# Attention with squared relu, then a gated feed-forward block: the first batch's queries loaded and transposed by themselves, and the order of the early work changed

## The chip, the core and the metric

The kernel runs on one core of a Trainium2 chip. A core has a matrix engine (TensorE, PE in the profile; its weight loads are the row PEld), a vector engine (VectorE, DVE), a scalar engine (ScalarE, ACT), a general engine (GpSimd, POOL) and a synchronising engine (SyncE, SP). Each has its own instruction stream and works through it in order; semaphores between the streams do the waiting. Data comes from HBM into the on-chip SBUF by DMA; matrix products land in PSUM. The metric is the device time of one execution, in microseconds (us).

## The reference

There are 8 batches (B), 12 heads (H), a sequence of 448 (S), a head width of 64 (D); the model width DM is 768 and the feed-forward width F is 1536.

```
scores = scale * (q @ k.T)               # per batch and head, 448 x 448
attn   = max(scores, 0)**2 / 448
x      = attn @ v                        # heads side by side: 3584 x 768
xn     = x / sqrt(mean(x*x) + 1e-6) * rms_g
out    = (silu(xn @ w_gate) * (xn @ w_val)) @ w_out      # 3584 x 768
```

All inputs are float32; the kernel converts them to bfloat16 while it loads them.

## The kernel before

**Loads.** Every input is loaded by a DMA that GpSimd issues (`load_q`, `load_k`, `load_kx`, `load_v`, `load_vx`, `load_gv`, lines 89 to 136). Queries come in pairs of batches: partitions 0 to 63 of the tile `qld` hold the even batch (e = 0), partitions 64 to 127 the odd one (e = 1), and `load_q` issues one DMA for each. Keys and values are split into the first 384 rows (`kld`, `vld`) and the last 64 (`kxld`, `vxld`). Lines 138 to 167 set the order of the first loads: heads 0 and 1, then 2 and 3, then 4 to 7, then 8 to 11, each time the queries of both batches of the pair; then the first 256 columns of the gate and value weights (`load_gv(0, 256)`), the keys of batch 1, more weights, the values of batch 1, more weights. Later loads are issued from inside the loop.

**Transposes.** For the scores, queries and keys are needed with the head width on the partitions. `transposes(n)` does one pair of heads j of batch b, with n = 6b + j. For the first pair of batches, and for the queries of the second pair, it does so on TensorE: 14 small matmuls against an identity for the queries (`psQ`, both batches of the pair at once), 6 and 2 for the keys (`psK`), then one copy by VectorE each (lines 206 and 218) into `QT` and `KT`. Later batches are transposed by DMAs that SyncE issues.

**The loop.** Step m (lines 464 to 486) works on a third of a batch, four heads: b, t = m divided by 3. `scores(m, slots)` makes seven slots of scores; of each slot TensorE makes four matmuls in pairs (line 265), ScalarE takes the relu out of PSUM (line 273, two PSUM buffers), VectorE squares (line 274). `attend(m - 1)` multiplies the seven squared slots of the step before with the values (line 297), ScalarE scales the result (line 309) and VectorE squares it (line 310). Slots 0 to 2 use head pair 2t, slots 3 to 5 head pair 2t + 1.

**The feed-forward work.** After a batch's three steps `norm(b)` sums the squares over the model width on TensorE (line 331), takes the root on ScalarE (line 339) and appends eleven steps to a list `bg`: four reciprocals (line 352), six scalings (line 355), which write the six parts of `xn`, and `ready`, which calls `gates`. `gates` appends 24 pieces to the list `pieces`: for each of 12 blocks of the width F a `gate` piece (six matmuls of line 382, then silu) and a `val` piece (six matmuls of line 396, then a product on VectorE, line 403). After an odd batch, `outproj` appends 14 output pieces (line 425).

**What sets the order.** The whole order is written out by hand. Every engine runs its instructions in the order in which the loop emits them. `fill(us)` adds its budget to a running `debt`, emits pieces while the debt is positive (a gate or value piece counts as 1.13, an output piece as 1.97), and after each piece it runs one step of `bg`. With no piece left, it runs three steps of `bg` and sets the debt to zero. Three fills a step share a rate of 7.8 in steps 0 to 6 and of 13.8 from step 7 on.

Of the kernel before, what the change touches and what calls it, by code (L numbers as in the profile page):

```python
# [9 lines left out]
BF16 = mybir.dt.bfloat16  # L10
# [5 lines left out]
def kernel(  # L16
# [11 lines left out]
    nc = tc.nc  # L28
    P = nc.NUM_PARTITIONS

    B, H, S, D = q.shape
# [5 lines left out]
    XT0 = NCH * P  # L37
    XK = S - XT0

    NU = 7  # L40
    HALF = S // NU
# [4 lines left out]
    ND = HP // 2  # L46
# [5 lines left out]
    wpool = ctx.enter_context(tc.tile_pool(name="weights", bufs=1))  # L52
    ldpool = ctx.enter_context(tc.tile_pool(name="ld", bufs=2))
    tpool = ctx.enter_context(tc.tile_pool(name="tsb", bufs=2))
    rpool = ctx.enter_context(tc.tile_pool(name="relu2", bufs=10))
    xpool = ctx.enter_context(tc.tile_pool(name="xT", bufs=2))
    hpool = ctx.enter_context(tc.tile_pool(name="hT", bufs=14))
    opool = ctx.enter_context(tc.tile_pool(name="ostage", bufs=2))
    psum = ctx.enter_context(
        tc.tile_pool(name="psum", bufs=2, space=bass.MemoryType.PSUM)  # L60
    )
# [12 lines left out]
    q_t, k_t, kx_t, v_t, vx_t = {}, {}, {}, {}, {}  # L74

    def q_tile(pr):
        shape = [P, H, NU, D] if pr < 2 else [P, NU, H, D]
        q_t[pr] = ldpool.tile(shape, BF16, name="qld", tag="qld", bufs=1)

    def k_tile(b):  # L80
        shape = [P, H, NCH, D] if b < 2 else [P, NCH, H, D]
        k_t[b] = ldpool.tile(shape, BF16, name="kld", tag="kld")
        kx_t[b] = ldpool.tile([XK, H, D], BF16, name="kxld", tag="kxld")

    def v_tile(b):
        v_t[b] = ldpool.tile([P, H, NCH, D], BF16, name="vld", tag="vld")
        vx_t[b] = ldpool.tile([P, H, D], BF16, name="vxld", tag="vxld")

    def load_q(pr, h0=0, h1=H):
        for e in range(2):  # L90
            dst = q_t[pr][e * HALF : (e + 1) * HALF]
            src = q[2 * pr + e, h0:h1]
            if pr < 2:
                nc.gpsimd.dma_start(  # L94
                    out=dst[:, h0:h1],
                    in_=src.rearrange("h (p u) d -> p h u d", u=NU),
                )
            else:
                nc.gpsimd.dma_start(
                    out=dst, in_=src.rearrange("h (p u) d -> p u h d", u=NU)  # L100
                )

    def load_k(b, h0=0, h1=H):
        src = k[b, h0:h1, 0:XT0]
        if b < 2:
            nc.gpsimd.dma_start(
                out=k_t[b][:, h0:h1],
                in_=src.rearrange("h (p c) d -> p h c d", c=NCH),
            )
        else:  # L110
            nc.gpsimd.dma_start(
                out=k_t[b][:], in_=src.rearrange("h (p c) d -> p c h d", c=NCH)
            )

    def load_kx(b, h0=0, h1=H):
        nc.gpsimd.dma_start(
            out=kx_t[b][:, h0:h1], in_=k[b, h0:h1, XT0:S].rearrange("h p d -> p h d")
        )

    def load_v(b, h0=0, h1=H):  # L120
        nc.gpsimd.dma_start(  # L121
            out=v_t[b][:, h0:h1],
            in_=v[b, h0:h1, 0:XT0].rearrange("h (p c) d -> p h c d", c=NCH),
        )

    def load_vx(b):

        for t in range(2):
            nc.gpsimd.dma_start(
                out=vx_t[b][t * XK : (t + 1) * XK],  # L130
                in_=v[b, :, XT0:S].rearrange("h p d -> p h d"),
            )

    def load_gv(lo, hi):
        nc.gpsimd.dma_start(out=wg_sb[:, :, lo:hi], in_=wg_d[:, :, lo:hi])
        nc.gpsimd.dma_start(out=wv_sb[:, :, lo:hi], in_=wv_d[:, :, lo:hi])

    q_tile(0)
    k_tile(0)
    v_tile(0)  # L140
    load_q(0, 0, 2)
    load_k(0, 0, 2)
    ident = const_pool.tile([P, P], BF16, name="ident", tag="ident")
    masks.make_identity(nc, ident[:])
    load_kx(0)
    load_q(0, 2, 4)
    load_k(0, 2, 4)
    load_v(0, 0, 4)
    ones_bf = const_pool.tile([P, P], BF16, name="ones_bf", tag="ones_bf")
    nc.vector.memset(ones_bf[:], 1.0)  # L150
    eps_col = const_pool.tile([P, 1], FP32, name="eps_col", tag="eps_col")
    nc.vector.memset(eps_col[:], eps)
    for h0, h1 in ((4, 8), (8, 12)):
        load_q(0, h0, h1)
        load_k(0, h0, h1)
        load_v(0, h0, h1)
        if h0 == 4:
            load_vx(0)
    load_gv(0, 256)
    k_tile(1)  # L160
    load_k(1)
    load_kx(1)
    load_gv(256, 512)
    v_tile(1)
    load_v(1)
    load_vx(1)
    load_gv(512, 768)


# [2 lines left out]
    def step():  # L172
        if bg:
            bg.pop(0)()


    QT, KTt, R, XT, X2 = {}, {}, {}, {}, {}

    def big(pr=None, b=None):

        if pr is not None:
            QT[pr] = tpool.tile([P, HP, NU, P], BF16, name="QT", tag="QT")
        if b is not None:
            KTt[b] = tpool.tile([P, HP, S], BF16, name="KT", tag="KT")

    def turn(dst, src, rows):

        for hh in range(2):
            nc.tensor.transpose(  # L189
                out=dst[hh * D : (hh + 1) * D],  # L190
                in_=src(hh),
                identity=ident[:rows, :rows],
            )

    def transposes(n):


        b, j = divmod(n, HP)
        pr, e = divmod(b, 2)
        if pr < 2 and e == 0:  # L200
            if j == 0:
                big(pr, None)
            ps = psum.tile([P, NU, P], BF16, name="psQ", tag="rot", bufs=4)
            for u in range(NU):
                turn(ps[:, u, :], lambda hh: q_t[pr][:, 2 * j + hh, u, :], P)
            nc.vector.tensor_copy(out=QT[pr][:, j], in_=ps[:])
        if b < 2:
            if j == 0:
                big(None, b)
            ps = psum.tile([P, S], BF16, name="psK", tag="rot", bufs=4)  # L210
            for c in range(NCH):
                turn(
                    ps[:, c * P : (c + 1) * P],
                    lambda hh: k_t[b][:, 2 * j + hh, c, :],
                    P,
                )
            turn(ps[:, XT0:S], lambda hh: kx_t[b][:, 2 * j + hh, :], XK)
            nc.vector.tensor_copy(out=KTt[b][:, j], in_=ps[:])
        if j == 2 and b > 0 and b + 1 < B:
            if e == 1 and pr > 0:  # L220
                big(pr + 1, None)
                for u in range(NU):
                    nc.sync.dma_start_transpose(
                        out=QT[pr + 1][:, :, u, :],
                        in_=q_t[pr + 1][:, u].rearrange("p h d -> p (h d)"),
                    )
            big(None, b + 1)
            for c in range(NCH):
                nc.sync.dma_start_transpose(
                    out=KTt[b + 1][:, :, c * P : (c + 1) * P],  # L230
                    in_=k_t[b + 1][:, c].rearrange("p h d -> p (h d)"),
                )
            nc.sync.dma_start_transpose(
                out=KTt[b + 1][:, :, XT0:S],
                in_=kx_t[b + 1][:].rearrange("p h d -> p (h d)"),
            )
        if j == HP - 1:
            if b + 2 < B:
                k_tile(b + 2)
                load_k(b + 2)  # L240
                load_kx(b + 2)
            if e == 0 and pr + 1 < B // 2:
                q_tile(pr + 1)
                load_q(pr + 1)
            if b == 0:
                load_gv(768, 1024)
                load_gv(1024, F)
# [195 lines left out]

    debt = 0.0

    def fill(us):

        nonlocal debt
        debt += us
        if not pieces:  # L450
            for _ in range(3):
                step()
        while pieces and debt > 0:
            cost, fn = pieces.pop(0)
            fn()
            debt -= cost
            step()
        if not pieces:
            debt = 0.0


    N = B * ND
    transposes(0)
    for m in range(N + 1):
        rate = 7.8 if m < 2 * ND + 1 else 13.8
        if m < N:
            scores(m, (0, 1))
        if m > 0:
            attend(m - 1)
        else:  # L470
            transposes(1)
        if m < N:
            scores(m, (2, 3))
        if m + 1 < N:
            transposes(2 * m + 2)
        fill(0.36 * rate)
        if m > 0 and m % ND == 0:
            norm(m // ND - 1)
        if m < N:
            scores(m, (4, 5))  # L480
        if m + 1 < N:
            transposes(2 * m + 3)
        fill(0.36 * rate)
        if m < N:
            scores(m, (6,))
        fill(0.28 * rate)
    while pieces or bg:
        fill(4.0)

# [29 lines left out]
```

## Time and profile before

| | |
|---|---|
| median of 3 runs | 476.51 us (476.38, 476.51, 478.22) |
| the profiled execution | 478.51 us, its span 476.7 us |
| TensorE busy in the span | 450.5 us (94%) |
| VectorE, ScalarE busy | 252.1 us (53%), 253.1 us (53%) |
| GpSimd (DMA issue) busy | 70.4 us (15%) |
| read from and written to HBM | 48.76 MB, 11.01 MB |
| mean granted TensorE clock | 0.981 |

The span is the time from the first to the last instruction on the engines; the profiled execution's own time is 1.8 us more. A row of the timeline gives the start and the length of a group of instructions, the engine, the line, the output and the inputs, and in brackets how long the engine had been idle before and what ended that. The granted clock is the share of full speed at which TensorE was allowed to run.

### The profile page before, as it was taken

To read this page: it belongs to the slowest core of one execution; us is meant where nothing else is said; L and a number is where in the kernel's file an instruction comes from. 1 tells how busy PE (TensorE), PEld (TensorE's weight loads), DVE (VectorE), ACT (ScalarE), POOL (GpSimd) and SP (SyncE) were. 2 spreads that over 40 slices of the span, in tenths; PEclk is the share of its full clock that TensorE was granted. 3 is DMA by queue.
4 is the path that set the end of the run, shared out by engine and by line. 5 is a ranking of instruction groups with operands and counts; after the bars stand their busy time and mean duration, and the time that the engine had idled before them with its cause. 6 is when DMAs were issued, how large, how long until landed. Compare 5 with 4: busy or idle time off the path is not lost.

```text
span 476.7 us, 7190 instructions
## 1 busy us (share of the span) xinstructions
PE 450.5 (94%) x2904; PEld 221.3 (46%) x2904; DVE 252.1 (53%) x422; ACT 253.1 (53%) x365; POOL 70.4 (15%) x78
## 2 busy tenths in 40 slices
PE   4777699999999999999999999999999999999996
PEld 2332244444445554444445554444445554555563
DVE  2585846885456444955466434865456443722111
ACT  2498557846665447746564547746566445222110
POOL 9753223130210007100220002000000000000000
PEclk9997689999999999999999999999999999999999
DMA  9999999999793239970391229000002210000022
GB/s 102 184 192 174 187 174 202 177 129 112 140 136 76 100 94 129 138 114 7 64 119 67 100 84 109 0 1 0 2 0 82 86 67 1 0 1 0 34 99 100
DMA packets 129329, 42.74 MB, mean 90 GB/s; under 512 B 113424, under 2 KB 125712, under 8 KB 129296
## 3 DMA queue, kind: packets, MB, share of 16 engines
q0 software_dynamic: 96384, 24.38, 64.3%
q1 hardware_dynamic: 32912, 17.90, 15.6%
q8 instruction: 22, 0.36, 0.3%
q14 instruction: 11, 0.09, 0.1%
HBM read 48.76 MB, written 11.01 MB: 125 GB/s over the span
## 4 chain that ended last, share of the span: by engine, by line
PE 85%; ACT 5%; DVE 5%; DMA 2%; POOL 1%; issue 1%; ACTq 0%; DVEq 0%; POOLq 0%
PE psG L382 22%; PE psO L425 22%; PE psV L396 22%; PE psAV L297 8%; PE psS L265 7%; ACT r L273 3%; DVE r L274 2%; DMA kld<-in_k_dram 2%; PE psSS L331 1%; DVE rstd L352 1%; DVE xn L355 1%; PE psQ L189 1%; POOL qld L94 1%; DVE hT L403 1%; ACT rstd L339 0%
## 5 line engine op out<-in xcount | busy, mean ns | idle before, releaser
L273 ACT ACTIVATE r<-psS 128x896 bf16<-128x896 f32 x168 | 145.4, 925 | 41.5 <-PE psS L265 41.5
L274 DVE TENSOR_TENSOR r<-r 128x896 bf16<-128x896 bf16 x168 | 104.1, 623 | 86.0 <-ACT r L273 85.4
L382 PE MATMUL psG<-xn,wg_sb 128*128 128x448 bf16 x576 | 127.9, 357 | 3.3 <-DVE xn L355 3.1
L396 PE MATMUL psV<-xn,wv_sb 128*128 128x448 bf16 x576 | 126.0, 355 | 0.0
L425 PE MATMUL psO<-wo_sb,hT 128*128 128x384 bf16 x672 | 113.5, 326 | 1.0 <-DVE hT L403 1.0
L390 ACT ACTIVATE sig<-psG 128x448 bf16<-128x448 f32 x96 | 52.3, 546 | 108.8 <-PE psG L382 100.4
L403 DVE TENSOR_TENSOR hT<-sig,psV 128x448 bf16<-128x448 bf16 x96 | 59.1, 616 | 69.4 <-PE psV L396 67.5
L425 PEld LDWEIGHTS <-hT 128*128 128x128 bf16 x672 | 64.2, 98 | 48.1 <-issue 4.8
L396 PEld LDWEIGHTS <-wv_sb 128*128 128x128 bf16 x576 | 54.9, 98 | 57.0 <-issue 8.5
L382 PEld LDWEIGHTS <-wg_sb 128*128 128x128 bf16 x576 | 55.1, 99 | 56.3 <-issue 8.4
L265 PE MATMUL psS<-QT,KT 64*128 64x448 bf16 (+1 forms) x384 | 53.6, 373 | 9.0 <-ACT r L273 8.1
L434 ACT COPY ost<-psO 128x384 f32<-128x384 f32 x28 | 13.4, 478 | 57.0 <-PE psO L425 49.4
L436 DVE COPY ost<-psO 128x384 f32<-128x384 f32 x28 | 15.6, 556 | 43.0 <-PE psO L425 43.0
L121 POOL DMA_DIRECT2D vld<-in_v_dram x10 | 9.5, 952 | 174.3 <-PE psAV L297 168.0
L297 PE MATMUL psAV<-r,vld 128*64 128x448 bf16 x288 | 35.2, 385 | 0.0
L265 PEld LDWEIGHTS <-KT 64*128 64x128 bf16 (+1 forms) x384 | 14.2, 97 | 40.7 <-issue 37.4
L355 DVE SCALAR_TENSOR_TENSOR xn<-xT,g_sb,rstd 128x448 bf16<-128x448 bf16 x48 | 31.1, 678 | 0.1
L309 ACT ACTIVATE xT<-psAV 128x448 bf16<-128x448 f32 x48 | 23.5, 542 | 8.2 <-PE psAV L297 8.0
L352 DVE RECIPROCAL rstd<-rstd 128x112 f32<-128x112 f32 x32 | 25.4, 826 | 1.1 <-ACT rstd L339 1.1
L297 PEld LDWEIGHTS <-vld 128*64 128x64 bf16 x288 | 15.2, 116 | 17.4 <-issue 9.9
L310 DVE TENSOR_TENSOR x<-xT 128x896 bf16<-128x896 bf16 x24 | 15.0, 625 | 12.8 <-ACT xT L309 12.8
L189 PE MATMUL psQ<-ident,qld 128*64 128x128 bf16 x168 | 8.8, 260 | 6.7 <-DMA qld<-in_q_dram 6.7
(32 smaller groups left out, 148.5 us busy)
## 6 DMA issues: line engine op xcount, KB each, us to landing
out_dram<-ost SPq DMA_DIRECT2D x28, 384.0 KB, 2.3
kld<-in_k_dram POOLq DMA_DIRECT2D x7, 576.0 KB, 15.5
vld<-in_v_dram POOLq DMA_DIRECT2D x7, 576.0 KB, 8.5
qld<-in_q_dram POOLq DMA_DIRECT2D x6, 672.0 KB, 14.4
wo_sb<-in_moe_w_out_dram POOLq DMA_DIRECT2D x3, 768.0 KB, 24.5
vxld<-in_v_dram POOLq DMA_DIRECT2D x16, 96.0 KB, 9.6
wg_sb<-in_moe_w_gate_dram POOLq DMA_DIRECT2D x4, 384.0 KB, 12.9
wv_sb<-in_moe_w_val_dram POOLq DMA_DIRECT2D x4, 384.0 KB, 13.2
```

What stands on the lines that cost most here:

```text
L265: nc.tensor.matmul(out=ps[rows, hh, :S].rearrange("k (u x) -> k u x", u=NU), lhsT=kt[prt, j, keys], rhs=qt[prt, j, :, b % 2 * HALF : (b % ...
L273: nc.scalar.activation(out=r[:], in_=ps[:, :, :S], func=ACT.Relu)
L274: nc.vector.tensor_tensor(out=r[:], in0=r[:], in1=r[:], op=ALU.mult)
L297: nc.tensor.matmul(out=acc[i][hh * D : (hh + 1) * D, :], lhsT=w[rows, hh, :], rhs=r[rows, hh, :], start=(c == 0), stop=(c == NCH),)
L309: nc.scalar.mul(out=xt[:, i, :], in_=acc[i][:], mul=inv_attn)
L352: nc.vector.reciprocal(out=rstd[:, sl], in_=rstd[:, sl])
L355: nc.vector.scalar_tensor_tensor(out=xn[:, kt, :], in0=xt[:, kt, :], scalar=g_sb[:, kt : kt + 1], in1=rstd[:], op0=ALU.mult, op1=ALU.mult,)
L382: nc.tensor.matmul(out=ps[:], lhsT=wg_sb[:, kt, fb * P : (fb + 1) * P], rhs=xn[:, kt, :], start=(kt == 0), stop=(kt == KT - 1),)
L390: nc.scalar.activation(out=sig[:], in_=ps[:], func=ACT.Silu)
L396: nc.tensor.matmul(out=ps[:], lhsT=wv_sb[:, kt, fb * P : (fb + 1) * P], rhs=xn[:, kt, :], start=(kt == 0), stop=(kt == KT - 1),)
L403: nc.vector.tensor_tensor(out=HT[pr, fb][:, :, e * HALF : (e + 1) * HALF], in0=st["sig"][:].rearrange("p (u x) -> p u x", u=NU), in1=ps[:] ...
L425: nc.tensor.matmul(out=ps[:], lhsT=HT[pr, fk][:, u, :], rhs=wo_sb[:, fk, o * OW : (o + 1) * OW], start=(fk == 0), stop=(fk == FT - 1),)
```

## The change

Six things are changed.

- The first loads take only the queries of batch 0 (e = 0); those of batch 1 come as one DMA after all of batch 0, ahead of the keys of batch 1. The first weights come after the keys of batch 1 and not ahead of them, the second after the values of batch 1. A tile `qld` now has two buffers and not one. To make room, `relu2` has 9 buffers and not 10, `hT` 13 and not 14.
- For the first pair of batches `transposes` does the queries of one batch at a time, on 64 partitions: 14 matmuls of 64 columns and a copy of half the width, once for each batch.
- In the loop `transposes(2m + 2)` is emitted after slots 4 and 5 (it was after slots 2 and 3), `transposes(2m + 3)` after slot 6 (it was after slots 4 and 5).
- In step 3 (`first`) no fill is emitted; at its end all eleven steps of `norm(0)` are emitted in one run.
- In step 4 one more fill stands between slots 0 and 1 and `attend(3)`.
- In `fill` the three steps of `bg` for an empty list come after the pieces and not before them.

```diff
-    rpool = ctx.enter_context(tc.tile_pool(name="relu2", bufs=10))
+    rpool = ctx.enter_context(tc.tile_pool(name="relu2", bufs=9))
-    hpool = ctx.enter_context(tc.tile_pool(name="hT", bufs=14))
+    hpool = ctx.enter_context(tc.tile_pool(name="hT", bufs=13))
...
-        q_t[pr] = ldpool.tile(shape, BF16, name="qld", tag="qld", bufs=1)
+        q_t[pr] = ldpool.tile(shape, BF16, name="qld", tag="qld")
...
-    load_q(0, 0, 2)
+    load_q(0, 0, 2, (0,))
     load_k(0, 0, 2)
     ident = const_pool.tile([P, P], BF16, name="ident", tag="ident")
     masks.make_identity(nc, ident[:])
+    load_q(0, 2, 4, (0,))
     load_kx(0)
-    load_q(0, 2, 4)
     load_k(0, 2, 4)
     load_v(0, 0, 4)
...
-    for h0, h1 in ((4, 8), (8, 12)):
-        load_q(0, h0, h1)
-        load_k(0, h0, h1)
-        load_v(0, h0, h1)
-        if h0 == 4:
-            load_vx(0)
-    load_gv(0, 256)
+    load_q(0, 4, 8, (0,))
+    load_k(0, 4, 8)
+    load_vx(0)
+    load_v(0, 4, 8)
+    load_q(0, 8, 12, (0,))
+    load_k(0, 8, 12)
+    load_v(0, 8, 12)
     k_tile(1)
+    load_q(0, 0, H, (1,))
     load_k(1)
     load_kx(1)
-    load_gv(256, 512)
+    load_gv(0, 256)
     v_tile(1)
     load_v(1)
     load_vx(1)
+    load_gv(256, 512)
     load_gv(512, 768)
...
-        if pr < 2 and e == 0:
-            if j == 0:
+        if pr == 0 or pr == 1 and e == 0:
+            r0, r1 = (e * HALF, (e + 1) * HALF) if pr == 0 else (0, P)
+            if j == 0 and e == 0:
                 big(pr, None)
-            ps = psum.tile([P, NU, P], BF16, name="psQ", tag="rot", bufs=4)
+            ps = psum.tile([P, NU, r1 - r0], BF16, name="psQ", tag="rot", bufs=4)
             for u in range(NU):
-                turn(ps[:, u, :], lambda hh: q_t[pr][:, 2 * j + hh, u, :], P)
-            nc.vector.tensor_copy(out=QT[pr][:, j], in_=ps[:])
+                turn(ps[:, u, :], lambda hh: q_t[pr][:, 2 * j + hh, u, :], r0, r1)
+            nc.vector.tensor_copy(out=QT[pr][:, j, :, r0:r1], in_=ps[:])
...
-    def fill(us):
+    def fill(us, idle_steps=3):
         nonlocal debt
         debt += us
-        if not pieces:
-            for _ in range(3):
-                step()
         while pieces and debt > 0:
             cost, fn = pieces.pop(0)
             fn()
             debt -= cost
             step()
         if not pieces:
             debt = 0.0
+            for _ in range(idle_steps):
+                step()
...
     for m in range(N + 1):
         rate = 7.8 if m < 2 * ND + 1 else 13.8
+        first = m == ND
         if m < N:
             scores(m, (0, 1))
+        if m == ND + 1:
+            fill(0.36 * rate)
         if m > 0:
             attend(m - 1)
         else:
             transposes(1)
         if m < N:
             scores(m, (2, 3))
-        if m + 1 < N:
-            transposes(2 * m + 2)
-        fill(0.36 * rate)
+        if not first:
+            fill(0.36 * rate)
         if m > 0 and m % ND == 0:
             norm(m // ND - 1)
         if m < N:
             scores(m, (4, 5))
         if m + 1 < N:
-            transposes(2 * m + 3)
-        fill(0.36 * rate)
+            transposes(2 * m + 2)
+        if not first:
+            fill(0.36 * rate)
         if m < N:
             scores(m, (6,))
-        fill(0.28 * rate)
+        if m + 1 < N:
+            transposes(2 * m + 3)
+        if first:
+            while bg:
+                step()
+        else:
+            fill(0.28 * rate)
```

## The prediction

> **What bounds the kernel now.** I read the page first, then the busy time by stage, then what TensorE (PE) waited for, then the timeline around the two places that the change rewrites, step 4 and step 7.
>
> ```profile
> span 476.7 us, 7190 instructions
> ...
> PE 450.5 (94%) x2904; PEld 221.3 (46%) x2904; DVE 252.1 (53%) x422; ACT 253.1 (53%) x365; POOL 70.4 (15%) x78
> ...
> PE   4777699999999999999999999999999999999996
> ...
> PEclk9997689999999999999999999999999999999999
> ```
>
> ```profile
> 0.00:63.00 63.00, 43.02 (x348) 18.45 (x348) 36.81 (x69) 37.09 (x48) 33.92 (x48) 0.86 1.49 168
> 63.00:110.00 47.00, 45.99 (x360) 21.53 (x356) 32.94 (x55) 32.41 (x46) 13.45 (x10) 1.00 1.88 169
> 110.00:470.00 360.00, 358.96 (x2190) 180.04 (x2187) 181.82 (x298) 183.10 (x272) 23.08 (x20) 1.00 0.55 65
> ```
>
> The first numbers of a row are the length and PE's busy time, the last three the clock granted to PE, the DMA share and GB/s. From 63 us on PE is idle for 2.1 us in all: it is the bound, and the end comes when its work is done. Before 63 us it is idle for 20 us and part of its work runs at half clock. So a change is worth what it takes out of the first 63 us, less any hole that it opens in the full stretch.
>
> ```profile
> PE psS L265 <- ACT r L273: 8.1, 13, 2.0
> PE psQ L189 <- DMA qld<-in_q_dram: 6.7, 2, 5.0
> PE psG L382 <- DVE xn L355: 3.1, 3, 1.4
> ```
>
> PE's early waits are three: scores for a free PSUM buffer (ScalarE bound), transposes for queries, gates for `xn`. The timeline of PE in step 4 shows the last:
>
> ```profile
> 49.07 0.38 PE L297 MATMUL psAV<-r,vxld 64*64 64x448 bf16 x4
> 49.39 0.55 PE L265 MATMUL psS<-QT,KT 64*128 64x448 bf16 x4
> ...
> 53.05 0.93 PE L382 MATMUL psG<-xn,wg_sb 128*128 128x448 bf16 x2
> 54.66 1.73 PE L382 MATMUL psG<-xn,wg_sb 128*128 128x448 bf16 x3 [0.68 <-DVE xn L355]
> 57.82 0.53 PE L382 MATMUL psG<-xn,wg_sb 128*128 128x448 bf16 x1 [1.43 <-DVE xn L355]
> 58.14 2.45 PE L396 MATMUL psV<-xn,wv_sb 128*128 128x448 bf16 x6
> 60.38 2.45 PE L382 MATMUL psG<-xn,wg_sb 128*128 128x448 bf16 x6
> ```
>
> The first gate ends at 58.35, and two pieces at half clock (2.24 each on the chain that ended last) bring PE to 62.83. From 63 on such a piece takes 1.14.
>
> ```profile
> 33.00:34.00 1.00, 0.59 (x10) 0.30 (x9) 0.82 (x3) 1.00 (x2) 0.59 (x1) 1.00 1.58 194
> 34.00:35.00 1.00, 0.59 (x10) 0.33 (x7) 0.85 (x3) 1.00 (x3) 0.46 (x1) 1.00 1.61 193
> 35.00:36.00 1.00, 0.53 (x4) 0.20 (x3) 0.99 (x3) 1.00 (x2) 0.29 (x1) 0.73 1.83 179
> ```
>
> Here the clock falls to half after some 3 us of PE busy a little over half the time, with no gap over 1 us.
>
> **Start, 0 to 37 us.** The first scores wait for `kxld`, issued at 3.83, landed 3.4 us later. In the new order its issue comes after two single query DMAs (0.66 and 0.62) in place of one double (1.32), and 320 KB are ahead of it as before: no change, 8.0. Query loads of 112, 112 and 224 KB for batch 1 leave the way of the keys of heads 4 to 7; those landed at 15.75 (8.45 + 7.3), and at the 0.6 us that 112 KB took they now land near 13. More, slots 4 and 5 of step 0 no longer stand behind `transposes(2)`, for which PE waited 1.75 and 0.69. So relu 4 and 5 follow relu 3 directly: 14.95 for the end of relu 5, before 18.81. Slot 6 and the transposes follow, and `attend(0)` starts near 17.4, before 20.70: 3.3 us gained.
>
> Now the moved transposes cost. Their VectorE copies (0.38 alone, 0.30 when queued) come after the squares of slots 4 and 5, and the next step's slot 0 needs them; now there are two, QT and KT. ScalarE ends relu 6 about 0.7 us before that slot's scores are there; this occurs at the start of steps 1, 2 and 3, in place of no gap. With relus 0.81 apart, `attend` at 3.0 cold and 1.6 warm and xT 0.98, xT(0) begins at 20.5 (23.71), xT(1) at 28.35 (30.76), xT(2) between 36.25 and 37.45 (39.19), depending on the clock. I take 2.3 us gained at xT(2), its end 37.85. The 6 half-width query transposes of batch 1 (about 0.42 each on PE, set by 14 weight loads of 30 ns) and their 6 copies lie beside ScalarE in steps 2 and 3. The halves of batch 0 save 0.24 us of VectorE each, hidden too.
>
> **Norm in one run, 37 to 53 us.** From the end of xT(2) to the end of the root took 3.56 us (40.17 to 43.73): the same again, 41.4. Relus 4, 5, 6: 43.9. VectorE: square 5 at 43.7, two copies 44.3, square 6 44.85, two copies 45.45, four reciprocals (0.76 apart) 48.5, six scalings (0.60 apart) 52.1. The first gate ends at 52.65, before at 58.35: 5.7 earlier. But behind that gate on PE stand `attend(3)` and all that ScalarE waits for next: PE has not yet done `attend(3)` (1.57), slots 2 to 5 of step 4 (0.97), and transposes 10 and 11 (2 x (0.51 + 0.42)): 4.4 us. Two pieces at half clock follow in both. Net 1.3 us gained. From PE's idle time of 4 us ahead of the gates the clock is certain to be low there.
> Both ends: with the copies hidden, the clock full in `attend(0)`, xT(2) at its early end and both pieces at 1.14, 2.1 + 1.4 + 0.6 + 2.2 more, at most 7.6 in all; with xT(2) late and the clock back 1.5 us later, a loss of 0.8. Nearest is the step 4 shown, cold until 62.7, so 1.3.
>
> **The list runs dry in step 7.** This is counted from the code. Before, step 4 emits 5 pieces, steps 5 and 6 emit 7 each (7.8/1.13), and 5 of the 24 of batch 0 remain for step 7; they carry the last scalings of `norm(1)`. With the change step 4 emits 10 (3 + 2 + 3 + 2), steps 5 and 6 seven each: exactly 24. `norm(1)` is queued in step 6 with 5 pieces left, its steps run with them as four reciprocals and one scaling, three more scalings follow at the end of step 6, two and `ready` in the first fill of step 7. The first gate of batch 1 comes only in the second fill, after slots 4 and 5 and a query transpose.
> Counted from the end of `attend(6)` on PE (A): slots 2 and 3 (0.5), then two xT (0.98) and two relus (1.75) until slot 5 is free at 2.75, its scores, the transpose (0.5): PE is at the gate at A + 3.5. VectorE has by then a queue from step 6: squares 4 and 5, a copy (0.54), four reciprocals (3.0), three products (0.53 each), square 6, a copy, four scalings (2.4) end near A + 1.8; then five squares, then the two scalings, at A + 5.7. The gate ends at A + 6.0. PE's own work in that time is 2.6 (0.97 scores, 0.5, 1.14): 3.4 us idle. In this stretch PE is some 40% busy, less than at 33 to 36, so the clock falls; the rise costs as at 58: 2 x (2.24 - 1.14) = 2.2. The 1.0 us that the gate waited here before (104.37 behind a scaling) goes. Sum 4.6 lost.
> Bounds: without the VectorE queue and with a full clock A + 4.6, that is 2.0 idle, 1.0 lost; like step 4 (49.45 to 58.35, 8.9) 6.3 idle, 7.5 lost. I take 4.6, between them, worked out from the queue.
> The page TensorE: Matmul & The Clock Gate of the Trainium skill ("Why this matters for your kernels") says that idle gaps under about 3 us keep the clock; the longest here is 1.4, and by that rule the loss would be 2.4. The fall at 35.7 speaks against it.
>
> **Later steps.** The queue is 3 to 5 pieces shorter throughout: in steps 13 and 19 the last scaling comes only one or two pieces before the gate. By the same count the gate waits 0.3 and 0.9: 1.2 lost; none to two thirds more is possible (0 to 2).
>
> **Costed at nothing.** `relu2` and `hT` with one buffer fewer: slot 2's buffer is read by `attend`, which PE passes anyway; `hT` is next written after the output pieces on PE. Weights: columns 1024 on landed at 69 to 73 us, their gate comes near 78; if they were late, up to 2 us. GpSimd: the queries of the third pair no longer wait 14.6 us (101.26); nothing behind them was late. The loads that `transposes(2m + 3)` issues keep their order among GpSimd's loads. SyncE: the transposing DMAs of step 3 waited for the keys until 48.2 and are used in step 6, past 80.
>
> **Sum.** -1.3 + 4.6 + 1.2 = +4.5. The profiled execution took 478.51 (span 476.7 and 1.8 around it), so 483.0 for such a one; it is 2.0 above the median, so against the median 481.0.
>
> **Rivals.**
> The clock decides, on the other side. If PE, denser from 13 us on, keeps full clock in `attend(0)`, `attend(2)`, the first pieces and step 7, 1.4 + 0.6 + 2.2 + 2.2 go: 6.4, so 474.6, with the copies hidden too 472.5. It ends below before from 4.5 us of clock loss saved. For it: `attend(0)` follows 4 us of dense work. Against: before, every stretch half busy lost the clock. 0.16.
> A small hole in step 7. If the clock holds there, 2.2 go: 478.8; if VectorE has no queue either, 3.6: 477.4. Neither is seen as a change. For it: VectorE is 70% busy from 63 to 110. Against: the recorded 1.0 us wait in the same step, with fewer scalings in a row, and the fall at 35.7. The skill's rule on gaps, above, speaks for 478.8. 0.18.
> The start does not pay. If the copies and the late `attend(3)` eat the gain (0.8 lost, not 1.3 gained) and step 7 is like step 4 (7.5), with 1.2 later, it is +9.5: 486.0. 0.11.
> The forecast has the rest, 0.55.
>
> **Numbers.** No change is told from one of 0.5% (2.4 us) here, so faster is below 474.1. Of the clock case 0.10 lies there and 0.06 within, with the small hole 0.24 within; the forecast and the last rival are slower, 0.66. The likeliest case by itself spans 479 to 485. The range reaches into the small-hole and clock cases and to the start that does not pay: 475.5 to 486.
>
> **What would show it.** Relu 5 of step 0 ending near 15; `attend(0)` near 17.4; ten norm steps back to back on VectorE, ending near 52; the first gate of batch 1 late, with PE idle and its clock at half in step 7 (around 90 to 105 us); PE waits on `xn` of about 1 us in two later steps. The forecast is wrong if PE has no hole past 63 us, or if the clock is full from 20 us on.

## The result and the profile after

The changed kernel takes 481.02 us (median of 4 runs, 480.4 to 481.2), the kernel before beside it 477.35 (476.38 to 478.22, also 4): a ratio of 1.0075, with a 95% interval of 1.0047 to 1.0103. It is slower by some 3.6 us. The profiled execution of the changed kernel took 480.94, its span 479.2; that of before had a span of 476.7. So 2.5 us are to be found in the two traces.

The page of the changed kernel, the lines that answer to those of before:

```profile
span 479.2 us, 7358 instructions
...
PE 453.0 (95%) x2988; PEld 222.3 (46%) x2988; DVE 252.3 (53%) x428; ACT 253.6 (53%) x365; POOL 68.7 (14%) x75
...
PE   3886799989999999999999999999999999999996
...
PEclk9957599989999999999999999999999999999999
```

PE is busy 2.5 us longer, and the granted clock is low in slices 3 to 5 and once more in slice 9: a new place, 96 to 108 us. The busy time by stage of the changed kernel (length, PE busy, weight loads, VectorE, ScalarE, GpSimd, then clock, DMA share, GB/s):

```profile
0.00:63.00 63.00, 43.81 (x392) 18.44 (x392) 35.05 (x68) 36.31 (x46) 32.27 (x45) 0.78 1.47 167
63.00:110.00 47.00, 44.97 (x361) 21.31 (x360) 33.15 (x58) 31.52 (x45) 13.41 (x10) 0.96 1.87 177
110.00:470.00 360.00, 359.28 (x2209) 179.81 (x2208) 183.02 (x300) 185.32 (x274) 23.07 (x20) 1.00 0.52 64
```

The mean clock before 63 us fell from 0.86 to 0.78. (The clock is on record only from 21.05 us on, in the kernel before from 25.2 on, and the view counts the time ahead of that as full; the rows show half clock there: four score matmuls took 0.93 at 8.02 and 0.55 at 38.63.) From 63 to 110 PE idles for 2.0 us where it idled for 1.0, and its clock is 0.96 and not 1.00. After 110 it idles for 0.7, before for 1.0.

The waits of PE in the first 110 us of the changed kernel (sum, count, longest):

```profile
PE psS L269 <- ACT r L277: 6.8, 8, 1.6
...
PE psG L386 <- DVE xn L359: 3.8, 1, 3.8
...
PE psS L269 <- DVE KT L222: 3.4, 4, 1.1
```

The wait for queries is shorter (4.8, before 6.7), the three waits for `xn` are one long one, and the waits of the scores for the copies of `KT`, late now, have grown from 0.8 to 3.4: those ahead of slot 0 in steps 2 and 4 (0.83 and 0.99) are new.

PE's timeline of the changed kernel around steps 2 and 4:

```profile
26.53 2.45 PE L301 MATMUL psAV<-r,vld 128*64 128x448 bf16 x12
...
46.20 0.93 PE L269 MATMUL psS<-QT,KT 64*128 64x448 bf16 x4 [0.99 <-DVE KT L222]
...
50.95 3.51 PE L386 MATMUL psG<-xn,wg_sb 128*128 128x448 bf16 x6 [3.81 <-DVE xn L359]
54.25 2.44 PE L400 MATMUL psV<-xn,wv_sb 128*128 128x448 bf16 x6
56.49 2.34 PE L386 MATMUL psG<-xn,wg_sb 128*128 128x448 bf16 x6
58.76 1.33 PE L301 MATMUL psAV<-r,vld 128*64 128x448 bf16 x12
```

The first row is `attend(1)` at half clock. The gate waits 3.81 us, is then paced by the scalings, and the next two pieces take over 2.2 each. `attend(3)` starts only at 58.76; before, it was done by 49.4. What the gate waited for is on VectorE, ten steps back to back:

```profile
47.19 2.98 DVE L356 RECIPROCAL rstd<-rstd 128x112 f32<-128x112 f32 x4
50.21 3.66 DVE L359 SCALAR_TENSOR_TENSOR xn<-xT,g_sb,rstd 128x448 bf16<-128x448 bf16 x6
```

And the new hole, PE in step 7 of the changed kernel:

```profile
99.82 0.55 PE L269 MATMUL psS<-QT,KT 64*128 64x448 bf16 x4
101.77 0.36 PE L269 MATMUL psS<-QT,KT 64*128 64x448 bf16 x2 [1.39 <-ACT r L277]
102.58 0.36 PE L269 MATMUL psS<-QT,KT 64*128 64x448 bf16 x2 [0.45 <-ACT r L277]
102.87 0.90 PE L191 MATMUL psQ<-ident,qld 128*64 128x128 bf16 x14
103.70 2.88 PE L386 MATMUL psG<-xn,wg_sb 128*128 128x448 bf16 x6
106.41 1.30 PE L400 MATMUL psV<-xn,wv_sb 128*128 128x448 bf16 x6
```

The last matmul of that gate by itself:

```profile
106.10 0.47 PE L386 MATMUL psG<-xn,wg_sb 128*128 128x448 bf16 x1
```

Between slots 2, 3 and slots 4, 5 there is no piece to put, so PE waits for ScalarE to free the PSUM. The first gate of batch 1 begins at 103.70 and takes 2.71 to the next piece in place of 1.14. Its clock is half from 102.99 to 106.40, and its last two operands come late from VectorE:

```profile
99.72 2.46 DVE L359 SCALAR_TENSOR_TENSOR xn<-xT,g_sb,rstd 128x448 bf16<-128x448 bf16 x4
...
104.78 1.27 DVE L359 SCALAR_TENSOR_TENSOR xn<-xT,g_sb,rstd 128x448 bf16<-128x448 bf16 x2
```

The last scaling ends at 106.05, the last matmul starts at 106.10, and the next piece starts 0.31 later. At full clock that last stretch takes 0.19 (the second experiment below, 105.94 to 106.13). So the gate ended when the scalings let it, and the half clock made it about 0.1 later.

**Where the 2.5 us are.** First 63 us: before, PE had done the first gate, two more pieces, `attend(3)`, slots 2 to 5 and transposes 10 and 11 by 62.76. The changed kernel has the three pieces at 58.76 and needs 4.06 for the others by its own rows (1.58, 0.48, 0.48, 0.77, 0.75): 62.82. The first 63 us together are worth nothing: +0.06. Step 7: idle 1.39 and 0.45, 0.32 more for the transposes, 1.57 more for the gate, less the 1.0 that the gate waited here before: +2.7. Later idle time: -0.3. Sum +2.5.

### The profile page after: what moved, and what is told of

Read it like the earlier page. It is cut to its first block, busy times and chain, and to the rows that moved or that the text cites. A ratio compares the mean times of both kernels' runs of the same rounds, so it can differ in the third digit from the quotient of the medians.

```text
span 479.2 us, 7358 instructions
## 1 busy us (share of the span) xinstructions
PE 453.0 (95%) x2988; PEld 222.3 (46%) x2988; DVE 252.3 (53%) x428; ACT 253.6 (53%) x365; POOL 68.7 (14%) x75
## 4 chain that ended last, share of the span: by engine, by line
PE 87%; DVE 6%; ACT 4%; issue 1%; DMA 1%; POOL 0%; DVEq 0%; ACTq 0%; POOLq 0%
PE psO L429 23%; PE psV L400 22%; PE psG L386 22%; PE psAV L301 8%; PE psS L269 8%; ACT r L277 3%; DVE xn L359 2%; PE psSS L335 2%; DVE r L278 1%; DVE rstd L356 1%; PE psQ L191 1%; PE psK L191 1%; DMA kxld<-in_k_dram 1%; DVE hT L407 0%; DVE QT L209 0%
## 5 line engine op out<-in xcount | busy, mean ns | idle before, releaser
L386 PE MATMUL psG<-xn,wg_sb 128*128 128x448 bf16 x576 | 129.5, 359 | 5.1 <-DVE xn L359 4.5
L269 PE MATMUL psS<-QT,KT 64*128 64x448 bf16 (+1 forms) x384 | 54.9, 385 | 10.3 <-ACT r L277 6.8
L269 PEld LDWEIGHTS <-KT 64*128 64x128 bf16 (+1 forms) x384 | 14.1, 99 | 42.9 <-issue 37.9
L356 DVE RECIPROCAL rstd<-rstd 128x112 f32<-128x112 f32 x32 | 25.2, 822 | 0.0
L191 PE MATMUL psQ<-ident,qld 64*64 64x64 bf16 (+1 forms) x252 | 9.7, 223 | 4.8 <-DMA qld<-in_q_dram 4.8
```

What stands on the lines that cost most here:

```text
L269: nc.tensor.matmul(out=ps[rows, hh, :S].rearrange("k (u x) -> k u x", u=NU), lhsT=kt[prt, j, keys], rhs=qt[prt, j, :, b % 2 * HALF : (b % ...
L356: nc.vector.reciprocal(out=rstd[:, sl], in_=rstd[:, sl])
L386: nc.tensor.matmul(out=ps[:], lhsT=wg_sb[:, kt, fb * P : (fb + 1) * P], rhs=xn[:, kt, :], start=(kt == 0), stop=(kt == KT - 1),)
```

## Experiments

The theory, from the prediction: the start gains a little, the late `attend(3)` gives most of that back, and the list that runs dry in step 7 makes the loss. The rivals: the start itself does not pay, or the clock decides. Each ratio is to the kernel before, timed beside it (its medians in the three groups: 477.59, 477.76 and 476.62 us). A span is that of the one profiled execution, which need not be a typical one: that of the kernel before took 478.51, 1.2 above its median.

**One part alone: the start.** Loads, half transposes and late transposes of the change; norm steps and fills as before.

```diff
+    (loads, qld, transposes: as changed)
...
-        if m + 1 < N:
-            transposes(2 * m + 2)
         fill(0.36 * rate)
...
         if m + 1 < N:
-            transposes(2 * m + 3)
+            transposes(2 * m + 2)
         fill(0.36 * rate)
         if m < N:
             scores(m, (6,))
+        if m + 1 < N:
+            transposes(2 * m + 3)
         fill(0.28 * rate)
```

> Theory: the start (queries of batch 0 alone, half transposes, later transposes) gains little at xT(2) (0.5 us in the changed kernel) and the loss of the change lies in step 7, where the list of pieces runs dry. With the old fills and the old norm steps five pieces remain for step 7 and no hole opens there: span 475.5 to 477.5 (before 476.7, changed 479.2), the wait of the first gate of batch 1 stays near 1 us. Rival: the later transposes and the added half-width query transposes are what costs; then the span stays at 478.5 or more with no hole in step 7.

Measured: 479.19 us, ratio 1.0047 (1.0031 to 1.0063). `attend(0)` came at 17.45, 3.2 us earlier than before, but xT(2) at 39.24 (before 39.19), and the first gate ended at 59.3, 1 us later. In step 7 the gate of batch 1 waits 0.5 us and no hole opens. Its span of 476.9 lies in the range expected, but the range was set beside a span of before that belongs to an execution above the median; by the ratio the start gains nothing and costs about half a per cent, and in that the rival is right. Its trace has 27.3 us of half clock on record (8 stretches of 3.41), before has 17.1 (5).

**The other part alone: norm in one run, a fill ahead of `attend(3)`.** Loads and transposes as before. (In `fill` the three steps of `bg` come after the pieces, as in the change.)

```diff
+        first = m == ND
...
+        if m == ND + 1:
+            fill(0.36 * rate)
...
-        fill(0.28 * rate)
+        if first:
+            while bg:
+                step()
+        else:
+            fill(0.28 * rate)
```

> The old loads and transposes with the norm steps in one run and the fill ahead of attend(3). Theory: the first gate ends near 54.3 (before 58.35) but attend(3) and four slots are still to be done, 0.6 us gained; the list runs dry at the end of step 6, 2.8 us lost in step 7: span 478.5 to 479.5. Rival (the loss comes with the start): span at or under 477.

Measured: 480.5 us, 1.0054 (1.0031 to 1.0077), span 480.1 and so above the range expected. PE's timeline of this kernel in step 7:

```profile
102.72 0.93 PE L382 MATMUL psG<-xn,wg_sb 128*128 128x448 bf16 x4
105.35 0.35 PE L382 MATMUL psG<-xn,wg_sb 128*128 128x448 bf16 x1 [1.70 <-DVE xn L355]
105.94 0.38 PE L382 MATMUL psG<-xn,wg_sb 128*128 128x448 bf16 x1 [0.25 <-DVE xn L355]
106.13 2.43 PE L396 MATMUL psV<-xn,wv_sb 128*128 128x448 bf16 x6
108.36 1.89 PE L382 MATMUL psG<-xn,wg_sb 128*128 128x448 bf16 x6
```

The hole is here without any change to the start: a wait of 1.70 for scalings, and then two pieces at half clock, which take 2.23 and 1.72 from start to start where 1.14 is usual. It comes with the fills, as counted; the next experiment takes the extra one away.

**The changed kernel without the extra fill.**

```diff
-        if m == ND + 1:
-            fill(0.36 * rate)
```

> The changed kernel without the fill ahead of attend(3). Theory: attend(3) and slots 2 and 3 of step 4 run under the scalings, where TensorE was idle from 47.1 to 50.9: 2.0 us gained; three pieces are left at step 7, and its hole shrinks from 2.8 to about 0.5: span 474 to 475.5. Rival (the gates ahead are what pays, the hole is something else): span 479 or more, with the same idle time in step 7.

Measured: 475.01 us, 0.9956 (0.9940 to 0.9971), span 474.1. The two lines cost 5.1 us by span and 6.0 by the medians. PE's timeline of this kernel:

```profile
46.63 2.16 PE L301 MATMUL psAV<-r,vld 128*64 128x448 bf16 x12
...
49.24 0.93 PE L269 MATMUL psS<-QT,KT 64*128 64x448 bf16 x4
...
50.89 0.35 PE L386 MATMUL psG<-xn,wg_sb 128*128 128x448 bf16 x1 [0.72 <-DVE xn L359]
...
54.20 2.44 PE L400 MATMUL psV<-xn,wv_sb 128*128 128x448 bf16 x6
...
101.89 1.29 PE L400 MATMUL psV<-xn,wv_sb 128*128 128x448 bf16 x6
```

`attend(3)` and slots 2 and 3 run while VectorE is still at the scalings, and the gate ends at 54.4, no later than with the fill (54.46). The first value of batch 1 stands at 101.89, in the changed kernel at 106.41. Of the 5.1 us, 2.8 come from the first 63 us and 2.6 from step 7; 0.3 are lost later (waits of 1.0 and not 0.7). So the extra fill brought the gates nothing, held up what could have run beside the norm, and emptied the list early.

**Work to hold the clock before the first gate.** The changed kernel with 14 unused matmuls into the gate's own PSUM tile; they only occupy PE.

```diff
+            if b == 0 and fb == 0:
+                for _ in range(14):
+                    nc.tensor.matmul(out=ps[:], lhsT=wg_sb[:, 0, 0:P],
+                                     rhs=wg_sb[:, 1, 0:S], start=True, stop=True)
```

> The changed kernel with 14 more matmuls of 448 columns on TensorE right before the first gate, into the PSUM tile that the gate then overwrites; their result is not used. Theory (the clock is lost to TensorE's idle time from 45 to 51): dense work brings the clock back before the first gate ends, so the next two pieces take 1.14 each and not 2.24: 2.2 us gained, span 477; the hole in step 7 stays. Rival (the clock comes back no sooner, or the added work delays the gate): span 479 or more, both pieces at 2.24.

Measured: 478.78 us, 1.0051 (1.0031 to 1.0071), span 476.9. PE's timeline of this kernel:

```profile
46.93 4.09 PE L387 MATMUL psG<-wg_sb 128*128 128x448 bf16 x14
...
53.99 1.30 PE L409 MATMUL psV<-xn,wv_sb 128*128 128x448 bf16 x6
55.12 1.30 PE L395 MATMUL psG<-xn,wg_sb 128*128 128x448 bf16 x6
```

With PE busy in the wait, the next two pieces start 1.13 apart and not 2.24, and together take 2.4 and not 4.5. That is the 2.2 us of the prediction's two half-clock pieces; the span is 2.3 shorter. (The two ratios' intervals overlap, and three of this kernel's seven times are 480.3 to 480.8, so the rows carry this and not the medians.) The hole in step 7 stays.

**Late transposes alone, and loads alone.** The first kernel has only the two moved `transposes` calls of the first diff; the second has the loads and the half transposes with the loop of before.

> The kernel before with one edit: transposes(2m + 2) after slots 4 and 5, transposes(2m + 3) after slot 6. Theory: the place of the transposes brings the larger part of the early start (slots 4 and 5 of step 0 no longer wait for the loads of heads 4 to 7), attend(0) near 19.3 against 20.70 before and 17.13 in the changed kernel; but the copies ahead of the next step's slot 0 open gaps of 0.5 to 1 us on ScalarE in steps 1, 2 and 3, so xT(2) begins within 0.7 us of before (39.19). Time within 0.3% of before. Rival (loads bring the start): attend(0) stays at 20.5 or later, time 0.5% or more above before.

> The changed loads and half-width transposes with the old loop, old fills and old norm steps. Theory: the keys of heads 4 to 7 land near 13 and not 15.75, attend(0) near 18.2, and no gap opens on ScalarE at the step borders, so more of the gain is kept: xT(2) begins at 37.5 or earlier, time 0.2 to 0.5% below before. Rival (the added half-width query transposes and copies cost what the loads bring): xT(2) at 38.5 or later, time no lower than before.

Measured: late transposes 476.43 us, 0.9982 (0.9964 to 0.9999); loads 478.26, 1.0014 (0.9997 to 1.0031). Neither is told from the kernel before by half a per cent. With late transposes `attend(0)` came at 19.25, as expected, and xT(2) at about 37.9, earlier than expected, although PE waits 3.2 us for copies of `KT`. With the loads `attend(0)` came at 17.45, and then `attend(1)` at 26.03 ran at half clock (2.41); xT(2) came at 37.9, and the 0.2 to 0.5% expected of the loads did not come. Together, in the first experiment, they cost half a per cent that neither costs alone. The stretches of half clock on record are 6 and 7, together 8, before 5. But the late transposes have one more than before and are no slower, so that the half clock is the cause of this half per cent is not shown. (The smaller `relu2` and `hT` pools are in the kernel with the loads too; they alone do not cost it.)

**A longer list.** The changed kernel with fewer pieces in steps 5 and 6, so that some are left for step 7.

```diff
+        if m in (5, 6):
+            rate = 5.0
```

> The changed kernel with the rate of steps 5 and 6 at 5.0, so that five pieces are left for step 7. Theory: only the hole of step 7 shrinks, from 3.7 us of idle and half-clock time to about 1; 2 to 3 us gained against the changed kernel (481.0): 478 to 479. Rival (the hole is set by VectorE being behind, not by the list): the first gate of batch 1 waits as long as before, 480.5 or more.

Measured: 480.16 us, 1.0058 (1.0035 to 1.0082), span 479.2: next to nothing gained. PE's timeline of this kernel in step 7:

```profile
103.80 0.74 PE L386 MATMUL psG<-xn,wg_sb 128*128 128x448 bf16 x3
105.68 0.35 PE L386 MATMUL psG<-xn,wg_sb 128*128 128x448 bf16 x1 [1.14 <-DVE xn L359]
...
107.06 1.30 PE L400 MATMUL psV<-xn,wv_sb 128*128 128x448 bf16 x6
```

The clock holds now, yet the gate still waits, 1.14 and twice 0.25, for scalings that VectorE does only at 104.95 to 106.8. The list and VectorE's queue are two limits that lie close together: with one mended, the other sets the gate. I had expected 2 to 3 us, and that was wrong. By the rows PE loses 2.1 us in step 7 and not 3.7 (the 1.0 that it lost there before included). The span shows none of it: PE idles 0.6 more in step 5, where the lower rate leaves it less to do, 0.3 more after 110 us, and this execution's first scores came 1.1 later, behind `kxld`, of which 0.6 is left at `attend(3)`.

**Norm in one run, and nothing else.** The second experiment without the extra fill.

```diff
         (as in the second experiment)
-        if m == ND + 1:
-            fill(0.36 * rate)
```

> The old loads and transposes, norm steps in one run, no fill ahead of attend(3): the kernel of the third run with the old start. Theory: the start of the change is worth little, so this one is within 1 us of that run (475.0): 474.5 to 476. Rival (the start pays once the fill ahead is gone): 476.5 or more.

Measured: 473.86 us, 0.9906 (0.9876 to 0.9935): faster than both kernels, and 0.6 below the range expected. The profiled execution took 470.86 and is the fastest of its six, so its rows show the order better than the size: its `attend(0)`, with loads and transposes as before, came at 19.74 and ran at full clock (1.33), where before's came at 20.70 and took 2.45, and its xT(2) came at 36.80. PE's timeline:

```profile
44.30 2.40 PE L297 MATMUL psAV<-r,vld 128*64 128x448 bf16 x12
...
48.12 0.35 PE L382 MATMUL psG<-xn,wg_sb 128*128 128x448 bf16 x1 [0.18 <-DVE xn L355]
...
51.28 1.30 PE L396 MATMUL psV<-xn,wv_sb 128*128 128x448 bf16 x6
52.42 1.30 PE L382 MATMUL psG<-xn,wg_sb 128*128 128x448 bf16 x6
```

`attend(3)` lies under the norm steps, the gate follows the scalings one by one from 48.12, and the pieces behind it run at full clock 7 to 8 us ahead of before's (58.14, 60.38); 2.4 of that is the earlier xT(2). Against the second experiment, which differs by the extra fill alone, the ratio goes from 1.0054 to 0.9906. Against the third, which has the changed start besides, it goes from 0.9956 to 0.9906, and the intervals do not overlap: here too the start costs about half a per cent.

**Work to hold the clock in steps 1 and 2.** The changed kernel with five unused matmuls after slots 2 and 3 of steps 1 and 2; `dense` multiplies `ones_bf` and `KT` into a PSUM tile that nothing reads.

```diff
+        if m in (1, 2):
+            dense(m, 5)
```

> The changed kernel with five more matmuls of 448 columns, whose result is not used, after slots 2 and 3 of steps 1 and 2, where TensorE was idle for 1.0 us each time and its clock fell to half at 24.5 us until 38.1. Theory (the gain of the start was lost to that fall): the clock stays full through attend(1) or attend(2), which take 1.6 and not 3.0; xT(2) begins at 36 to 37.5 and not 38.7, and 1.5 to 2.5 us are gained against 481.0: 478.5 to 479.5. Rival (the copies and loads limit the start, not the clock): xT(2) stays at 38.5 or later, 480.5 or more.

Measured: 477.91 us, 1.0021 (1.0008 to 1.0034), span 475.9. PE's timeline of this kernel:

```profile
21.17 1.12 PE L451 MATMUL psD<-KT,ones_bf 128*128 128x448 bf16 x5
26.51 1.32 PE L301 MATMUL psAV<-r,vld 128*64 128x448 bf16 x12
28.57 1.12 PE L451 MATMUL psD<-KT,ones_bf 128*128 128x448 bf16 x5
34.20 1.33 PE L301 MATMUL psAV<-r,vld 128*64 128x448 bf16 x12
```

ScalarE's rows of xT(2): this kernel, the changed one, the one before:

```profile
35.88 0.98 ACT L313 ACTIVATE xT<-psAV 128x448 bf16<-128x448 f32 x2
38.73 0.98 ACT L313 ACTIVATE xT<-psAV 128x448 bf16<-128x448 f32 x2 [1.21 <-PE psAV L301]
39.19 0.98 ACT L309 ACTIVATE xT<-psAV 128x448 bf16<-128x448 f32 x2 [1.78 <-PE psAV L297]
```

Ten matmuls that compute nothing make the kernel 3.3 us faster by span (2.6 by the ratios). `attend(1)` and `attend(2)` run in 1.3, xT(2) begins at 35.88 and not at 38.73, and the first gate ends at 51.6 and not at 54.46. That is more than expected, and the start as the prediction had it (xT(2) between 36.25 and 37.45). It shows what ate it: the clock, from 24.46 on. The hole in step 7 stays here too, with half clock from 99.54 to 102.95.

**Can the best be bettered?** Three additions to the kernel with norm in one run: unused matmuls in steps 2 and 3 (six and nine), late transposes, and the changed loads.

> The kernel with the old start, norm steps in one run and no fill ahead (473.9), with more matmuls whose result is not used: six after transposes(6) in step 2 and nine after transposes(9) in step 3. Theory: the clock no longer falls near 33 and 43.5; attend(2) and attend(3) take 1.6 and not 2.8, 1 to 2.5 us gained: 471.5 to 473. Rival: the added matmuls stand ahead of slots that ScalarE waits for, or the clock falls anyway: 473.5 or more.

> The same kernel (old start, norm in one run, no fill ahead) with the later transposes alone. By themselves they took 0.2% off the kernel before; if the parts add, 472.5 to 473.5. Rival: what they gain is used up by the copies ahead of slot 0; 474 or more.

> The same kernel with the changed loads and half-width transposes alone, the transposes in their old place. By themselves they added 0.1% to the kernel before; if the parts add, 474 to 475. Rival: the earlier attend(0) now pays, since the first gate follows at once: 473 or less.

Measured: 473.41 us, 0.9923 (0.9902 to 0.9944); 473.28, 0.9921 (0.9904 to 0.9939); 473.04, 0.9927 (0.9904 to 0.9951). None is told from 0.9906; the first and the third missed what was expected of them, 471.5 to 473 and 474 to 475, by less than 1 us. In the first the clock stays full from 20.6 to 51.28 us, yet its time is not told from that without the matmuls: with `attend(3)` and the norm steps side by side, nothing was seen to be won by holding the clock up to there. One stretch of half clock follows, over the two pieces behind the gate. So 0.7 to 0.9% below before is what these parts give, and no more than the one run of norm steps gives by itself.

## Why the prediction was right, and where it was not

The forecast of 481.0 met the median of 481.02, and the direction and two of the three mechanisms held. But its sum was +4.5 between profiled executions, and the traces give +2.5: the start came out 1.4 worse, step 7 1.9 and the later steps 1.5 better than forecast. The time was still met, because before's profiled execution stands 1.2 above its median (477.35) and after's, 480.94, stands on its own, and because the median of before then known, 476.51 of three runs, lies 1.1 and 1.2 below two of the three later, longer series (0.1 below the third). So two misses of 2.0 us met, and that is luck: the agreement is closer than the working.

- **First scores 8.0, relu 5 at 14.95, `attend(0)` at 17.4.** Measured 8.02, 14.79, 17.13. Right, 3.6 us earlier than before; the loads alone bring 3.25 of it, the late transposes alone 1.45 (17.45 and 19.25 in the two experiments). The size is less sure than that: with the loads and transposes of before it came at 19.74 to 21.16 in different traces.
- **Late copies, 0.7 of idle ScalarE at the start of steps 1 to 3.** Right in kind: ScalarE idles 0.58, 1.10 and 0.54 there. Only at step 2 does PE wait for a copy of `KT` (0.83); at steps 1 and 3 its transposes, at half clock, fill the time.
- **2.3 us gained at xT(2).** Wrong: 0.46. The step that failed is "`attend` at 3.0 cold and 1.6 warm", of which I took the warm figure for `attend(1)`. The clock fell at 24.46, and it took 3.0, xT(1) began at 29.54 in place of 28.35, and half clock lasted to 38.11. The prediction had seen the clock fall in a half-busy stretch at 35.7 and did not ask the same of the stretch that it had itself made thin, 21 to 24 us. The experiment with ten matmuls in steps 1 and 2 returns 2.85 us at xT(2), so the cause is shown.
- **Norm in one run: reciprocals and scalings back to back, two pieces at half clock.** Right in shape: ten steps in 6.7 us, 1.8 later than forecast since xT(2) was. The pieces at half clock cost 2.2, as the experiment before the gate shows.
- **The late `attend(3)` gives back 4.4 us.** Right: 4.06 by rows. With the start at 0.46 the net gain of 1.3 became a loss of 0.06. What the prediction did not say is that the fill ahead has no use: without it the gate ends at the same time.
- **The list runs dry in step 7, gate at A + 6.0, 4.6 lost.** Right in kind and place: the gate ended at A + 6.6 (A is 99.82), behind the scalings that were named. The term for the clock was mis-sized: 2.2 by two pieces at half clock. In fact the half-clock stretch began at 102.99, inside the wait, and ended with the gate, so it cost about 0.1 at the gate's end; all the rest is waiting, 3.6 and not 3.4, less the 1.0 waited before: 2.7. Where the stretch began later against the gate, in the second experiment, the two pieces behind it paid 1.7 together.
- **The skill's rule on gaps.** The Trainium skill, page TensorE: Matmul & The Clock Gate ("Why this matters for your kernels"), asks for no idle gaps of PE above about 3 us, which the prediction read as: shorter gaps keep the clock; by that step 7 would have lost 2.4. The longest gap was 1.39 and the clock fell, so the trace contradicts that reading; its time came nearer than mine all the same (2.7), because the fall cost next to nothing.
- **Later steps, +1.2.** Wrong: -0.3. One wait for `xn` of 0.7, not two; and waits of 1.0 of the output pieces for `hT`, the products of VectorE, which the old order had, were gone.
- **Rivals.** "The start does not pay" had its first half right: the first experiment has the start alone slower by half a per cent. "A small hole in step 7" had the price nearly right (2.4, measured 2.7) and its condition wrong: the clock did not hold. "The clock decides, on the other side" was wrong in sign: the clock lost 9 stretches of 3.41 us, before 5 (against that, the half clock of the very start ended at 21.05 and not at 25.2). The two experiments with unused matmuls show what the clock was worth in two places, 2.3 and 3.3 us by span; neither made the kernel faster than the one before, and both together were not run.

## What to carry to other kernels

Before work is moved ahead of a wait, ask what else stands behind that wait on the engine: here two lines put a gate that could not start ahead of an `attend` that could, and cost 5 us, while norm in one run, by itself, was worth 0.9%. Count a hand-fed list to its end: a piece spent early is missing where it covered a wait, and a second queue may sit right behind the first. A stretch in which TensorE is thinned by a better order of loads can lose its clock, and then the gain is eaten one stage later.

## What the runs showed of the hardware that I had not expected

**Half clock comes in whole stretches of 3.41 us.** From 21.05 us on the changed kernel had it at 24.46 to 38.11, 44.94 to 58.59 and 102.99 to 106.40: 13.65, 13.65 and 3.41, which is 4, 4 and 1 times 3.41. All the other kernels' stretches are multiples too, apart from one that begins in the last 2.2 us of each span or just behind it; before had 1, 1 and 3. This agrees with the window of 3413 ns in the Trainium skill's page TensorE: Matmul & The Clock Gate (Part 1: The HAM clock gate).

**The clock falls behind windows that are thin, and not only behind long gaps.** Two windows of the changed kernel, the one before the fall and the first after it:

```profile
21.05:24.46 3.41, 2.04 (x50) 1.32 (x49) 2.57 (x5) 3.41 (x6) 0.83 (x1) 1.00 1.71 187
24.46:27.87 3.41, 2.58 (x20) 0.98 (x17) 2.91 (x7) 2.31 (x3) 1.61 (x2) 0.50 1.49 196
```

And in the kernel with unused matmuls in steps 1 and 2, the same first window and the one before its own fall at 41.52:

```profile
21.04:24.46 3.42, 2.93 (x47) 1.50 (x47) 2.40 (x4) 3.42 (x6) 0.83 (x1) 1.00 1.73 187
...
38.11:41.52 3.41, 1.67 (x32) 0.92 (x34) 1.10 (x3) 3.38 (x5) 1.65 (x2) 1.00 1.76 184
```

The second number is PE's busy time, the third from the end the clock. With 2.04 the clock was lost, with 2.93 kept, and with 1.67 lost. The longest gap ahead of the fall at 24.46 was about 1.0 us. The second row shows that 2.58 us of work at half clock did not bring the clock back; what does was not separated.

Busy time alone does not settle it. Here are a window that kept the clock (norm in one run with late transposes) and one that lost it (norm in one run with the changed loads):

```profile
41.67:45.08 3.41, 1.92 (x24) 0.92 (x25) 2.71 (x6) 2.79 (x4) 0.82 (x1) 1.00 2.40 160
```

```profile
30.62:34.03 3.41, 2.56 (x50) 1.48 (x45) 3.04 (x7) 3.41 (x5) 2.33 (x3) 1.00 1.85 182
```

In all fourteen traces, up to 110 us, every full-clock window with less than 1.9 us of PE lost the clock and every one with more than 2.6 kept it; in between both occur. What else counts is open. Transposes seem to count for something: with late transposes alone, a window from 22.53 us on kept the clock with 2.57 us of PE, 1.79 of them transposes, while 1.75 of gate matmuls alone lost it in the changed kernel without the extra fill (from 50.39 us on).
